# A routed MLP after sliding attention: the fourth unit's token rows gathered in quarters and turned by VectorE

## The chip, the cores and the metric

The kernel runs on one core of one Trainium2 chip. The metric is the device time of one execution in microseconds (us). The core has TensorE (matmuls), VectorE, ScalarE, GpSimd and SyncE, which run side by side and meet at semaphores, and sixteen DMA engines that move data between the chip's large memory (DRAM) and the on-chip memory.

## What is computed

Attention with two masks (a window of 32 keys, or every fourth key of the last 128), then a mixture of 8 experts of which each token uses one. A token whose local gate is 0.5 or more takes the expert of the token before it. Batch 8, 8 heads of 64, 576 tokens, so 4608 token rows of D = 512; an expert is 512 to 1024 to 512.

```python
scores = np.where(masks[None], scale * np.matmul(q, k.transpose(0, 1, 3, 2)), -1e9)
attn = softmax(scores)
x = (attn @ v) as (B, S, H * D)
logits, local_gate = x @ w_gate, sigmoid(x @ w_local)
for b in range(B):
    prev_e = -1
    for s in range(S):
        fresh_e = argmax(logits[b, s])
        e = fresh_e if s == 0 or local_gate[b, s] < 0.5 else prev_e
        prev_e = e
        out[b, s] = softmax(logits[b, s])[e] * (relu(x[b, s] @ w1[e]) @ w2[e])
```

## The kernel before

**Stages.** For the first 150 us or so the kernel computes attention for 64 (batch, head) pairs and stores the rows x into a DRAM buffer `xd`. Routing (logits, the running expert, counts) is mixed in. Then come 24 *units* of the expert MLP, numbered from 0. Units 0 and 1 are formed early, from the first half of the tokens; all others are late, from all tokens. A *pair* unit holds two tiles of 128 tokens of one expert, a *full* unit one tile, a *half* unit 64 tokens. Units 0 to 4 and 6 are pairs, unit 5 is full. Weights sit in three slots; units 0, 2, 4 use slot 0, units 1, 3, 6 slot 1, unit 5 slot 2. The loop at L1333 runs, for each unit u: the first layer of u (`run_hidden`, L1268), the rows of u + 1 (`features`, L951), the gathers of u + 5, and the second layer of u - 1 (`run_output`, L1283).

**One layer of a pair** is seven products instead of eight (`chain`, L955): sums of weight blocks and of row blocks are made by VectorE (L869 to L878), TensorE makes the products in three banks x, y, z, and each bank is read out by `keep` (ScalarE) or `finish` (VectorE at L1037 for the first layer and L1118 for the second). Bank x collects several products; the last of them may only be added to it when VectorE's `finish` of the one before has read it.

**The rows of a unit** are gathered from `xd` by GpSimd's indirect DMAs (L910), a list of closures (`fetches`) that is worked off as the program is written out: each gap between products adds credit, and a gather costs 2 or 3 of it (`fetch_some`, L913). Whatever is missing is issued when the rows are needed (`fetch_all`, L921). Each gather is preceded by a one-element memset on VectorE (L909), for which GpSimd waits, so the place of that memset in VectorE's queue sets the earliest time of the gather.

**Two ways to turn rows.** A matmul needs rows with the features on the partitions. For units below `TURNED`, two gathers per tile of 128 tokens fetch half rows of 1 KB (256 features), by the indices `row0` and `row1`. TensorE turns them with four 128 by 128 transposes a tile (L942), and ScalarE copies the result (L943). For the other units, four gathers per tile fetch quarter rows of 512 bytes, by the indices `at`, each group of 32 partitions another quarter, so that VectorE's transpose of 32 by 32 squares (L936) puts everything in place by itself. The features then lie in another order, so these units use a second copy of the first weights, with its rows in that order (`w1[u >= TURNED]`, L821). A weight load is skipped when the slot already holds the expert (L826), except where the copy changes between a slot's two users (L822).

**When gathers are queued.** `late_tokens` (L1184) queues units FIRST to TURNED - 1 and `places` (L730), which computes `at`, queues units TURNED to 5. The rows of unit 3 are turned within the first layer of unit 2, after the fifth product (L1275).

VectorE's and TensorE's queues run in the order in which the program is written; nothing moves an instruction ahead later.

Of the kernel before, what the change touches and what calls it, by code (L numbers as in the profile page):

```python
# [73 lines left out]
EARLY, FIRST = 2, 2  # L74
# [7 lines left out]
KEPT = EARLY * GB * 2  # L82


TURNED = FIRST + 2

AHEAD = 4

# [117 lines left out]
def whole(ctx, tc, exact, bad, qk, v, wgl, w1, w2, con, msk, qmk, out, cst, wg, ones):  # L206
# [523 lines left out]
    def places():  # L730
# [13 lines left out]
        nc.vector.scalar_tensor_tensor(at, codes, a_code, high, Alu.mult, Alu.add)  # L744
        for u in range(TURNED, FIRST + AHEAD):
            gather(u)
# [54 lines left out]
    def of_unit(u, what, j=0, rows=P):  # L801
        return tiles[what, units[u]["late"]][:rows, units[u]["col"] + j:units[u]["col"] + j + 1]
# [8 lines left out]
    def weights(u, second):  # L811
# [8 lines left out]
        e, held = units[u]["expert"], units[u]["held"]  # L820
        w, s, pattern = (w2, raw2, "p m f -> p (m f)") if second else (w1[u >= TURNED], raw1, "p m k f -> p (m k f)")  # L821
        if not second and u >= TURNED and units[u]["before"] < TURNED:  # L822
            held = None
# [68 lines left out]
    def gather(u):  # L892


        for j, n in enumerate({"pair": (NQS, NQS), "full": (NQS,), "half": (ROW // SQ,)}[units[u]["kind"]]):
            for q in range(2 if u < TURNED else n):
                fetches.append((u, lambda u=u, j=j, q=q: fetch(u, j, q)))

    def fetch(u, j, q):
        late, col = units[u]["late"], units[u]["col"] + j  # L900
        if q == 0:
            shape = [P, 2, D // 2]
            xg[u, j] = (stage.tile(shape, F32, name="xg", bufs=8) if late else mw.tile(shape, F32, name="xg"))
        x = xg[u, j]
        if u < TURNED:
            to, of, place = x[:, q], xh if late else xh[:EARLY * GS * 2], of_unit(u, f"row{q}", j)
        else:
            to, of, place = x.rearrange("p g (q f) -> p (g q) f", f=P)[:, q], xq, tiles["at"][:, q, col:col + 1]
        nc.vector.memset(to[0:1, 0:1], 0.0)  # L909
        nc.gpsimd.indirect_dma_start(out=to, out_offset=None, in_=of,  # L910
                                     in_offset=bass.IndirectOffsetOnAxis(ap=place, axis=0))

    def fetch_some(time):  # L913

        since[0] = min(since[0] + time, 5)
        cost = 2 if fetches and FIRST <= fetches[0][0] <= TURNED else 3
        if fetches and since[0] >= cost:
# [502 lines left out]
```

## Time and profile before

| what | value |
|---|---|
| median of 3 runs | 655.15 us (655.09 to 656.98) |
| the profiled execution | 657.47 us |
| its span, first to last instruction | 655.7 us |
| mean granted TensorE clock | 0.995 |
| gathers of `xg` by GpSimd (L910) | 16 by `row`, 120 by `at` |
| weight loads (L827) | 48 issued, 2048 KB each |
| software DMA queue (gathers and stores) | 19.41 MB |

How to read the views: the chain of waits goes back from the last instruction to whatever released it, step by step. In the timeline each row is a start in us from the span's beginning, a length, an engine, a line of the program and what it writes and reads; in square brackets stand the idle time of that engine before it and what ended it. "PE" is TensorE, "DVE" VectorE, "ACT" ScalarE, "POOL" GpSimd, "SP" SyncE.

### The profile page before, as it was taken

To read this page: it belongs to the slowest core of one execution; us is meant where nothing else is said; L and a number is where in the kernel's file an instruction comes from. 1 tells how busy PE (TensorE), PEld (TensorE's weight loads), DVE (VectorE), ACT (ScalarE), POOL (GpSimd) and SP (SyncE) were. 2 spreads that over 40 slices of the span, in tenths; PEclk is the share of its full clock that TensorE was granted. 3 is DMA by queue.
4 is the path that set the end of the run, shared out by engine and by line. 5 is a ranking of instruction groups with operands and counts; after the bars stand their busy time and mean duration, and the time that the engine had idled before them with its cause. 6 is when DMAs were issued, how large, how long until landed. Compare 5 with 4: busy or idle time off the path is not lost.

```text
span 655.7 us, 14698 instructions
## 1 busy us (share of the span) xinstructions
PE 635.9 (97%) x5980; PEld 558.3 (85%) x5980; DVE 415.8 (63%) x963; ACT 177.9 (27%) x318; POOL 253.3 (39%) x242
## 2 busy tenths in 40 slices
PE   8999999998998999999999999999999999999995
PEld 7978898878887999999699998699997799997974
DVE  4758888888686486754819744639724749717451
ACT  3545444353111332212122112132112123112310
POOL 4332243124004646554755554427553443110011
PEclk9999999999998999999999999999999999999999
DMA  9999989497004698575624425544114555531201
GB/s 340 411 414 339 351 303 296 161 379 282 8 25 177 208 409 310 178 293 185 267 81 156 168 64 227 228 174 158 41 60 153 194 220 216 173 146 26 117 33 44
DMA packets 29020, 131.40 MB, mean 200 GB/s; under 512 B 4909, under 2 KB 15277, under 8 KB 23184
## 3 DMA queue, kind: packets, MB, share of 16 engines
q1 hardware_dynamic: 21200, 110.96, 45.4%
q0 software_dynamic: 7744, 19.41, 8.8%
q8 instruction: 49, 0.80, 0.5%
q14 instruction: 27, 0.22, 0.1%
HBM read 145.03 MB, written 19.40 MB: 251 GB/s over the span
## 4 chain that ended last, share of the span: by engine, by line
PE 84%; DVE 8%; DMA 4%; issue 2%; POOL 1%; ACT 0%; POOLq 0%; DVEq 0%
PE yp L1103 28%; PE hp L1027 26%; PE sc L325 6%; PE hp L1001 4%; PE pv L379 4%; PE yp L1091 4%; PE yp L1074 2%; PE hp L989 2%; PE tp L398 2%; DMA xg<-xd,row 2%; DMA kq<-in_qk_dram 1%; DMA vt<-in_v_dram 1%; PE ap L614 1%; DVE pr L331 1%; PE lp L428 1%
## 5 line engine op out<-in xcount | busy, mean ns | idle before, releaser
L910 POOL DMA_INDIRECT xg<-xd,at x120 | 136.4, 1137 | 140.5 <-DVE xg L909 114.3
L1062 POOL DMA_INDIRECT out_dram<-y,tok x36 | 48.6, 1351 | 122.2 <-DVE y L1118 65.0
L1037 DVE TENSOR_TENSOR h<-hp,h 128x512 f32<-128x512 f32 x45 | 31.0, 690 | 93.5 <-PE hp L1027 93.3
L1103 PE MATMUL yp<-sum,hc 128*128 128x256 f32 x384 | 88.5, 380 | 0.0
L1027 PE MATMUL hp<-xc,sum 128*128 128x128 f32 x720 | 85.6, 275 | 0.0
L1027 PEld LDWEIGHTS hp<-xc,sum 128*128 128x128 f32 x720 | 82.9, 192 | 0.1
L1103 PEld LDWEIGHTS yp<-sum,hc 128*128 128x128 f32 x384 | 72.8, 190 | 9.9
L1118 DVE SCALAR_TENSOR_TENSOR y<-yp,gate,y 128x256 f32<-128x256 f32 x48 | 23.2, 483 | 76.3 <-issue 46.1
L331 DVE SCALAR_TENSOR_TENSOR pr<-sc,mk 96x512 f32<-96x512 f32 x64 | 47.0, 748 | 23.0 <-PE sc L325 22.4
L1103 PE MATMUL yp<-raw,h 128*128 128x256 f32 x256 | 61.0, 381 | 0.0
L334 ACT ACTIVATE pr<-pr 96x512 f32<-96x512 f32 x64 | 43.8, 684 | 58.6 <-DVE pr L331 57.0
L325 PE MATMUL sc<-kq 64*96 64x64 f32 x1152 | 56.7, 248 | 2.4 <-issue 1.4
L1027 PE MATMUL hp<-xe,raw 128*128 128x128 f32 x480 | 58.8, 276 | 0.0
L1027 PEld LDWEIGHTS hp<-xe,raw 128*128 128x128 f32 x480 | 56.5, 192 | 1.9 <-issue 1.6
L325 PEld LDWEIGHTS sc<-kq 64*96 64x96 f32 x1152 | 52.1, 161 | 6.9 <-issue 3.0
L274 POOL COPY vt<-vt 32x585 f32<-32x585 f32 x48 | 33.5, 699 | 62.2 <-DMA vt<-in_v_dram 43.2
L1103 PEld LDWEIGHTS yp<-raw,h 128*128 128x128 f32 x256 | 47.4, 190 | 9.1 <-issue 3.2
L1031 ACT COPY h<-hp 128x512 f32<-128x512 f32 x45 | 26.3, 585 | 73.4 <-PE hp L1027 73.4
L1038 ACT ACTIVATE h<-h 128x512 f32<-128x512 f32 x45 | 28.4, 630 | 63.4 <-DVE h L1037 48.5
L379 PE MATMUL pv<-vt,pr 128*64 128x65 f32 x1152 | 41.9, 225 | 2.0 <-issue 1.6
L379 PEld LDWEIGHTS pv<-vt,pr 128*64 128x64 f32 x1152 | 37.0, 137 | 4.5 <-issue 1.9
L1111 ACT ACTIVATE y<-yp,gate 128x256 f32<-128x256 f32 x48 | 22.7, 473 | 59.9 <-PE yp L1103 59.9
(224 smaller groups left out, 955.6 us busy)
## 6 DMA issues: line engine op xcount, KB each, us to landing
raw<-in_w_dram SPq DMA_DIRECT2D x48, 2048.0 KB
kq<-in_qk_dram SPq DMA_DIRECT2D x13, 1184.0 KB
vt<-in_v_dram SPq DMA_DIRECT2D x15, 880.0 KB
xd<-x SPq DMA_DIRECT2D x16, 512.0 KB
kq<-in_qk_dram SPq DMA_DIRECT2D x6, 592.0 KB
xg<-xd,at POOLq DMA_INDIRECT x120
xd<-x SPq DMA_DIRECT2D x32, 32.0 KB
vt<-in_v_dram SPq DMA_DIRECT2D x1, 585.0 KB
```

Source lines behind the costliest of these rows:

```text
L274: nc.gpsimd.tensor_copy(t[k * WIN:(k + 1) * WIN, VQ:], t[KW:, k * NB * VW:(k + 1) * NB * VW])
L325: nc.tensor.matmul(sc[:KW, u, (i - a) * QB:(i - a + 1) * QB], lhsT=kt[h, i * QB:i * QB + KW], rhs=qt[h, i * QB:(i + 1) * QB], start=True, ...
L331: nc.vector.scalar_tensor_tensor(to, sc[:KW, :, :w], -CEIL, mk[:, at:at + w].unsqueeze(1).to_broadcast([KW, 2, w]), Alu.max, Alu.min)
L334: nc.scalar.activation(to, to, Act.Exp, scale=SCALE)
L379: nc.tensor.matmul(pv[half * QB:(half + 1) * QB, k - a], lhsT=pr[:, u, (i - a) * QB:(i - a + 1) * QB], rhs=vt[:, u, i], start=True, stop=T ...
L910: nc.gpsimd.indirect_dma_start(out=to, out_offset=None, in_=of, in_offset=bass.IndirectOffsetOnAxis(ap=place, axis=0))
L1027: nc.tensor.matmul(to[:, m], lhsT=a[:, m, kk], rhs=b[:, kk], start=first and m == 0 and kk == 0, stop=(kk == DK // 2 - 1), skip_group_chec ...
L1031: nc.scalar.copy(at((0, 1, 3)[k]), of)
L1037: nc.vector.tensor_tensor(at(k), of, at(k), op=Alu.add)
L1038: nc.scalar.activation(at(k), at(k), Act.Relu)
L1062: nc.gpsimd.indirect_dma_start(out=rows_of_out(), out_offset=bass.IndirectOffsetOnAxis(ap=of_unit(u, "tok", j), axis=0), in_=y, in_offset= ...
L1103: nc.tensor.matmul(to, lhsT=a[:, m], rhs=b[:, m], start=first and m == 0, stop=(m == FK // 2 - 1), skip_group_check=True)
```

## The change

One constant moves. `TURNED` is the number of the first unit whose rows come in quarters; it goes from 4 to 3, so that unit 3, the fourth, changes sides.

```diff
-TURNED = FIRST + 2
+TURNED = FIRST + 1
```

It acts in six places. `gather` queues eight quarter gathers for unit 3 instead of four half gathers (the bytes are the same, 256 KB). `fetch` takes its indices from `at`, so its gathers are queued in `places` and no longer in `late_tokens`. `turn_rows` turns unit 3 with two VectorE transposes instead of eight TensorE transposes and two ScalarE copies. `weights` loads unit 3's first weights from the second copy, without the condition on the expert, and unit 6's with it. `fetch_some` charges unit 4's gathers 3 instead of 2.

On VectorE, within the first layer of unit 2. `h` is that layer's result, read out of the banks `hp`; `xc` and `xe` belong to unit 3's rows. Before, `xg_3060` and `xg_3109` are the two tiles of unit 4:

```order
L1037 TENSOR_TENSOR h_3047<-hp_3050,h_3047 128x4x128
L876 TENSOR_TENSOR sum_1_2509<-raw2_0_78,sum_1_2509 128x1024
L909 MEMSET xg_3060 1x1
L1037 TENSOR_TENSOR h_3047<-hp_3048,h_3047 128x4x128
L909 MEMSET xg_3109 1x1
L1037 TENSOR_TENSOR h_3047<-hp_3049,h_3047 128x4x128
L909 MEMSET xg_3109 1x1 x2
L875 TENSOR_TENSOR xc_3152<-xe_3112 128x256
```

After the change, where `xg_2996` and `xg_3059` are the tiles of unit 3 and `xg_3108` is the first of unit 4:

```order
L1037 TENSOR_TENSOR h_3046<-hp_3049,h_3046 128x4x128
L876 TENSOR_TENSOR sum_1_2509<-raw2_0_78,sum_1_2509 128x1024
L909 MEMSET xg_3059 1x1
L1037 TENSOR_TENSOR h_3046<-hp_3047,h_3046 128x4x128
L909 MEMSET xg_3108 1x1
L936 STREAM_TRANSPOSE xe_3111<-xg_2996 128x4x128
L936 STREAM_TRANSPOSE xe_3111<-xg_3059 128x4x128
L1037 TENSOR_TENSOR h_3046<-hp_3048,h_3046 128x4x128
L909 MEMSET xg_3108 1x1 x2
L875 TENSOR_TENSOR xc_3141<-xe_3111 128x256
```

The two transposes stand between the second and the third addition, and the memsets there belong to tiles of one place earlier.

On VectorE, within the first layer of unit 3, up to the transposes of unit 4's rows. Before, with `xg_3193` the tile of unit 5 and `xg_3253` the first of unit 6:

```order
L877 TENSOR_TENSOR sum_1_2509<-raw2_0_78 128x1024
L909 MEMSET xg_3193 1x1
L871 TENSOR_TENSOR hc_2511<-h_3047 128x512
L909 MEMSET xg_3193 1x1
L1037 TENSOR_TENSOR h_3166<-hp_3169,h_3166 128x4x128
L872 TENSOR_TENSOR hc_2511<-h_3047,hc_2511 128x512
L909 MEMSET xg_3193 1x1
...
L878 TENSOR_TENSOR sum_1_2509<-raw2_0_78,sum_1_2509 128x1024
L909 MEMSET xg_3253 1x1
L936 STREAM_TRANSPOSE xe_3260<-xg_3060 128x4x128
L936 STREAM_TRANSPOSE xe_3260<-xg_3109 128x4x128
```

After, with `xg_3108` and `xg_3192` the tiles of unit 4:

```order
L877 TENSOR_TENSOR sum_1_2509<-raw2_0_78 128x1024
L909 MEMSET xg_3108 1x1
L871 TENSOR_TENSOR hc_2511<-h_3046 128x512
L909 MEMSET xg_3192 1x1
L1037 TENSOR_TENSOR h_3155<-hp_3158,h_3155 128x4x128
L872 TENSOR_TENSOR hc_2511<-h_3046,hc_2511 128x512
...
L878 TENSOR_TENSOR sum_1_2509<-raw2_0_78,sum_1_2509 128x1024
L909 MEMSET xg_3192 1x1
L936 STREAM_TRANSPOSE xe_3246<-xg_3108 128x4x128
L936 STREAM_TRANSPOSE xe_3246<-xg_3192 128x4x128
```

At this place the memsets that were those of units 5 and 6 are those of unit 4, up to the last, which stands directly ahead of the transposes that read its tile.

On GpSimd, the gathers and stores in the order in which they are issued, from the first gather of unit 3 on (`y` is the result of unit 1 that is stored). Before:

```order
L910 DMA xg_2996<-xd_67,row01_2883 128x256
L910 DMA xg_2996<-xd_67,row11_2884 128x256
L1062 DMA out_dram<-y_2923,tok0_2126 4608x512
L910 DMA xg_3032<-xd_67,row01_2883 128x256
L910 DMA xg_3032<-xd_67,row11_2884 128x256
L1062 DMA out_dram<-y_2924,tok0_2126 4608x512
L910 DMA xg_3060<-xd_67,at_2965 128x128 x4
L910 DMA xg_3109<-xd_67,at_2965 128x128 x4
```

After:

```order
L910 DMA xg_2996<-xd_67,at_2965 128x128 x2
L1062 DMA out_dram<-y_2923,tok0_2126 4608x512
L910 DMA xg_2996<-xd_67,at_2965 128x128 x2
L1062 DMA out_dram<-y_2924,tok0_2126 4608x512
L910 DMA xg_3059<-xd_67,at_2965 128x128 x4
L910 DMA xg_3108<-xd_67,at_2965 128x128 x4
L910 DMA xg_3192<-xd_67,at_2965 128x128 x4
```

Unit 3 takes the four places that unit 4's first tile had, and unit 4's two tiles follow four places later.

## The prediction

> **What bounds the kernel now.** First the shares of the page, then the chain of waits that ended last.
>
> ```profile
> span 655.7 us, 14698 instructions
> PE 635.9 (97%) x5980; PEld 558.3 (85%) x5980; DVE 415.8 (63%) x963; ACT 177.9 (27%) x318; POOL 253.3 (39%) x242
> PE 84%; DVE 8%; DMA 4%; issue 2%; POOL 1%; ACT 0%; POOLq 0%; DVEq 0%
> ```
>
> TensorE is busy 97% of the span and carries 84% of the chain. So TensorE time that goes is worth its length only where TensorE itself is what comes last, and a wait that reaches TensorE costs its full length. The chain in order of time (start, length, what) around units 2 and 3:
>
> ```profile
> 142.24 6.76 DMA xg<-xd,row
> ...
> 205.52 3.33 DMA xg<-xd,row
> ...
> 223.47 0.87 PE tp L942 x8
> 224.34 3.59 PE hp L1027 x32
> ...
> 238.32 0.62 DVE h L1037
> 238.98 2.05 PE hp L1027 x16
> 241.03 12.09 PE yp L1103 x56
> 253.12 12.50 PE hp L1027 x112
> ```
>
> The eight transposes of unit 3 (L942) are on the chain, 0.87 us. Between 228 and 239 the chain runs over VectorE, and from 238.98 on it stays on TensorE with units back to back: output of unit 2 at 241.03, hidden of unit 4 at 253.12. What is lost there is not won back.
>
> **The change, part by part.** *TensorE* loses the eight transposes, 0.87 us, and ScalarE their two copies, which nobody waits for after 228. *VectorE* gets two square transposes for unit 3, in its queue behind the second of unit 2's three additions at L1037 and ahead of the third. *GpSimd* issues eight gathers for unit 3 where it issued four, so every later gather moves four places back. The rows of VectorE (start, length, idle time before it and what ended it):
>
> ```profile
> 223.58 0.69 DVE L1037 TENSOR_TENSOR h<-hp,h 128x512 f32<-128x512 f32 x1
> 226.17 0.69 DVE L1037 TENSOR_TENSOR h<-hp,h 128x512 f32<-128x512 f32 x1 [1.90 <-PE hp L1027]
> 228.03 0.43 DVE L875 TENSOR_TENSOR xc<-xe 128x256 f32<-128x256 f32 x1 [1.16 <-PE hp L1027]
> 235.25 1.22 DVE L877 TENSOR_TENSOR sum<-raw 128x1024 f32<-128x1024 f32 x1
> 240.64 0.71 DVE L936 STREAM_TRANSPOSE xe<-xg 128x512 f32<-128x512 f32 x1
> 242.92 0.71 DVE L936 STREAM_TRANSPOSE xe<-xg 128x512 f32<-128x512 f32 x1 [1.58 <-DMA xg<-xd,at]
> 250.29 0.48 DVE L1118 SCALAR_TENSOR_TENSOR y<-yp,gate,y 128x256 f32<-128x256 f32 x1
> ```
>
> and of GpSimd's gathers:
>
> ```profile
> 223.89 0.94 POOL L910 DMA_INDIRECT xg<-xd,at  x1 [0.90 <-DVE xg L909]
> 235.94 1.35 POOL L910 DMA_INDIRECT xg<-xd,at  x1 [5.53 <-DVE xg L909]
> 241.83 0.94 POOL L910 DMA_INDIRECT xg<-xd,at  x1 [0.30 <-issue]
> ```
>
> *Unit 3.* Its two transposes cost 2 x 0.71 = 1.4 us, and the idle 1.90 + 1.16 us before 226.17 and 228.03 covers that, if the data is there. Counting GpSimd's queue, unit 3's eighth gather takes the place that starts at 223.89. Under light traffic a gather took 3.33 us from its start until TensorE had it (205.52). Its issue had taken 1.61 us of that and this one takes 0.94, so I take 2.66, and the second transpose starts at 226.55. The third addition then runs 227.25 to 227.9, and xc (L875) starts at 227.95 instead of 228.03. TensorE comes 0.87 us earlier and then waits for VectorE's sums, which come 0.1 us earlier: of the 0.87 us about 0.1 is left. The bounds: all of the 0.87 gained if the data is early, or a gather of the loaded kind (142.24: 6.76 us; and 235.94 to 242.92, 6.98 us), landing at 230.87 and making VectorE 4.2 us late. I stay with the light case, for the load between 225 and 230 is light (busy time of each engine in a stretch; the last three columns are TensorE's granted clock, the busy share of the DMA engines and GB/s):
>
> ```profile
> 200.00:205.00 5.00, 5.00 (x25) 4.41 (x24) 4.57 (x13) 0.95 (x2) 2.55 (x2) 1.00 0.83 350
> 225.00:230.00 5.00, 5.00 (x46) 4.87 (x45) 2.67 (x7) 1.97 (x5) 3.48 (x3) 1.00 0.39 85
> 235.00:240.00 5.00, 4.85 (x44) 4.66 (x43) 5.00 (x13) 1.66 (x3) 3.24 (x3) 1.00 0.98 416
> 240.00:245.00 5.00, 5.00 (x30) 4.51 (x29) 3.28 (x8) 1.77 (x4) 3.33 (x3) 1.00 1.00 411
> 245.00:250.00 5.00, 5.00 (x25) 4.41 (x24) 4.97 (x8) 0.48 (x2) 1.72 (x2) 1.00 1.02 415
> ```
>
> *Unit 4* is where I expect the price. Now only one of its eight gathers is late: it starts at 235.94, and VectorE waits 1.58 us for it, until 242.92. After the change five are left at that point. The first of them has its memset behind L877 (235.25 + 1.22), so it starts at about 236.5, and the last has its memset right ahead of the transposes. GpSimd's five starts from 235.94 to 241.83 lie (241.83 - 235.94) / 4 = 1.47 us apart, so the last of unit 4's starts at 236.5 + 5.9 = 242.4. From 235 to 250 the DMA engines are full with weights (0.98 to 1.02), so I take 6.5 us for the landing, just under the 6.76 and 6.98 measured under load, since the load ends near 250. The bounds are 3.33 and 6.98. It lands at 248.9, and VectorE's second transpose starts 6.0 us late (248.9 against 242.92).
>
> Who waits: behind it stand unit 4's xc and weight sums and then the additions of unit 2's output at L1118. The one at 250.29 ends at 250.77, and TensorE's last product of that output writes on in the bank that it reads:
>
> ```profile
> 249.51 1.89 PE L1103 MATMUL yp<-raw,hc 128*128 128x256 f32 x8
> 251.23 1.89 PE L1103 MATMUL yp<-sum,h 128*128 128x256 f32 x8
> ```
>
> The slack is 251.23 - 250.77 = 0.46 us. Six us later the addition ends at 256.75, and TensorE stands **256.75 - 251.23 = 5.5 us** behind, with nothing else in its queue. The 0.87 us that it saved lies ahead of that stall and is swallowed by it.
>
> *Clock.* After an idle stretch the granted clock can halve:
>
> ```profile
> 148.00:149.00 1.00, 0.00 (x0) 0.00 (x0) 1.00 (x2) 0.00 (x0) 0.00 (x0) 1.00 1.16 457
> 210.00:211.00 1.00, 1.00 (x4) 0.73 (x4) 0.85 (x3) 0.09 (x1) 0.00 (x0) 0.50 0.45 131
> ```
>
> and on TensorE just ahead of the second of them:
>
> ```profile
> 208.99 0.47 PE L942 MATMUL tp<-cst,xg 128*128 128x128 f32 x2 [1.43 <-DMA xg<-xd,row]
> 209.26 3.55 PE L1103 MATMUL yp<-raw,hc 128*128 128x256 f32 x8
> ```
>
> After 1.43 us idle eight matmuls took 3.55 us instead of 1.89, at a clock of 0.50; a similar pause around 148.5 left it at 1.00. A pause of 5.5 us is far longer than either, so I add 3.55 - 1.89 = **1.7 us**. The Trainium skill (TensorE: Matmul & The Clock Gate, Part 1) has the clock halve after an idle window of about 3.4 us that runs freely. By that rule a pause of 5.5 us would be hit in most phases but not in all, 1.7 us with or without; the trace shows a drop after less idle time than it asks for.
>
> *Priced at nothing:* unit 3's first weights come from the other half of the weight table, 2 MB either way; that this load runs now is seen in the 350 GB/s at 200 to 205. Its condition on the expert held goes, and unit 6's load gets one; by the reference's inputs the slot's experts are 1, 4 and 5, so both load in both kernels. If unit 6's were skipped, the load from 241 on would thin, which is the light rival below.
>
> **Sum.** 5.5 + 1.7 = 7.2 us, on the profiled execution's span of 655.7 (its time 657.47). The median of the runs, 655.15, lies 2.3 us under that execution's time, with nothing that the change touches in between, so I add to the median: **662.3 us**.
>
> **Rivals.**
>
> 1. *The clock holds.* Only the stall: 655.15 + 5.5 = 660.7. For it speaks the row at 148.
> 2. *The late gather lands as under light load.* 242.4 + 3.33 = 245.7, 2.8 us late, so the addition ends at 253.6 and TensorE loses 2.4 us, a pause too short to be sure of a slow clock: 657.5. Against it stand the three windows at 0.98 to 1.02. The Trainium skill (DMA: Bandwidth & Descriptors, Anatomy of one DMA) gives 2.0 us and the bytes over 436 GB/s, by its figure an estimate of 2.15 us for 64 KB, so this rival is its rule. The 6.98 us here speaks against it.
> 3. *VectorE is never late* (not slower). If unit 4's last gather had landed by 242.92 + 0.46 = 243.4, no wait would reach TensorE, and at most the 0.87 us would remain: 654.3. It decides at a landing 1.0 us after the start at 242.4. No gather quoted was that quick.
> 4. *Unit 3's own last gather comes late as well* (weights for unit 4 start early and load the queue). VectorE is 4.2 us late at xc, TensorE waits there with a slow clock (1.7), and unit 4's gathers move by the same 4.2: together some 4.2 + 7.2 = 11.4 us, 666.5. Against it speaks 0.39 at 225 to 230.
>
> **How the numbers follow.** The forecast 0.62, rival 1 0.13, rival 2 0.11, rival 3 0.05, rival 4 0.09. The range 657.0 to 664.5 takes in landings from 3.3 to about 8 us with and without the clock, and leaves out rival 3, the lower part of rival 2 and rival 4, together about 0.18. A measurement of this kernel tells some 0.3% (2 us) from no change, 653.2 to 657.1: within it lie most of rival 3 and a third of rival 2, 0.08; faster 0.02; slower 0.90.
>
> **What would show it.** Right: no L942 near 223; the second unit-3 transpose on VectorE ending near 227; a wait of several us at unit 4's L936 for DMA xg, ending near 249; TensorE's last product of unit 2's output (L1103, now at 251.23) waiting for VectorE's L1118 until near 257, then some 3 us at half clock, and from there on every unit at its old length. Wrong: L936 of unit 4 released before 244; TensorE idle at 228 to 231, which would be rival 4; or a new wait at units 5 or 6, whose gathers also shift but whose last memsets stand 18 and more rows of VectorE's queue ahead of their transposes.

## The result, and the profile after

| | kernel before | changed kernel |
|---|---|---|
| median, 4 runs each on one chip | 655.88 us (655.09 to 656.98) | 665.47 us (662.10 to 666.52) |
| profiled execution, its span | 657.47, 655.7 us | 665.62, 663.8 us |
| mean granted clock | 0.995 | 0.993 |

The ratio is 1.0137, with a 95% interval of 1.0113 to 1.0160. On the 655.15 us from which the forecast was made this is 664.1 us (662.6 to 665.6), a loss of 9.0 us where 7.2 was forecast. The changed kernel's own median, 665.47, lies 1.0 us over the upper end of the range. One execution of `eager` below, 929 us at a granted clock of 0.654, is left out of its times.

The shares of the page, after:

```profile
span 663.8 us, 14702 instructions
PE 640.4 (96%) x5972; PEld 562.4 (85%) x5972; DVE 417.7 (63%) x969; ACT 176.8 (27%) x316; POOL 255.0 (38%) x246
PE 81%; DVE 9%; issue 4%; DMA 3%; POOL 2%; ACT 0%; POOLq 0%; DVEq 0%
```

TensorE has fewer instructions and yet is busy 4.5 us longer. That is not the price of the change: 3.0 us of it lie in the attention scores (L325, 59.7 us against 56.7), which the change doesn't touch, and the changed kernel's second trace, `after_2`, has 56.7 there again. What counts is that its share of the chain falls from 84% to 81%: elsewhere it waits.

The chain of waits in order of time (start, length, what):

```profile
242.63 6.94 DMA xg<-xd,at
249.75 0.72 DVE xe L936
...
256.06 1.13 DVE sum L872
257.65 3.78 PE yp L1103 x8
261.43 13.04 PE hp L1027 x112
274.48 12.09 PE yp L1103 x56
...
625.24 12.09 PE yp L1103 x56
```

A gather (xg) has taken TensorE's place on the chain. The output of unit 4 starts at 274.48, and that of the last units at 625.24. In the chain of the kernel before:

```profile
265.63 12.09 PE yp L1103 x56
...
616.39 12.09 PE yp L1103 x56
```

Both are 8.85 us earlier there. So nothing is lost or won in the 350 us behind the first of them; all of it happens ahead of 274. (The spans differ by 8.1 us only, because from the issue of the last store to the end it takes 4.8 us here and 5.5 before.) TensorE, from the timeline (idle time and what ended it in brackets):

```profile
230.31 3.81 PE L1027 MATMUL hp<-xc,sum 128*128 128x128 f32 x32 [0.73 <-DVE sum L869]
...
250.05 1.89 PE L1103 MATMUL yp<-raw,hc 128*128 128x256 f32 x8
257.65 3.78 PE L1103 MATMUL yp<-sum,h 128*128 128x256 f32 x8 [5.71 <-DVE xg L909]
```

The last but one product of unit 2's output starts at 250.05, against 249.51 before. Up to there the two executions differ by 0.54 us only. That is a balance: the first product of any unit's output (L1103) starts 2.36 us later than before (168.27 against 165.91), before loses 1.66 us to its half clock near 209, and of the 0.87 us saved some 0.2 are left. The last product starts at 257.65; with before's distance of 1.72 us it would be 251.77, so **5.88 us** are lost at the stop. That product then takes 3.78 us instead of 1.89, and the first layer of unit 4 takes 13.04 instead of 12.50: **2.43 us** more. 0.54 + 5.88 + 2.43 = 8.85, of which 5.88 + 2.43 = 8.31 belong to the change.

The name in the bracket, the memset L909, is a neighbour in VectorE's queue; what TensorE waits for is seen in VectorE's own rows:

```profile
224.96 0.70 DVE L936 STREAM_TRANSPOSE xe<-xg 128x512 f32<-128x512 f32 x1
227.33 0.71 DVE L936 STREAM_TRANSPOSE xe<-xg 128x512 f32<-128x512 f32 x1 [1.67 <-issue]
228.56 0.42 DVE L875 TENSOR_TENSOR xc<-xe 128x256 f32<-128x256 f32 x1
...
244.51 0.71 DVE L936 STREAM_TRANSPOSE xe<-xg 128x512 f32<-128x512 f32 x1 [3.12 <-DMA xg<-xd,at]
249.75 0.71 DVE L936 STREAM_TRANSPOSE xe<-xg 128x512 f32<-128x512 f32 x1 [4.53 <-DMA xg<-xd,at]
...
255.58 0.48 DVE L1118 SCALAR_TENSOR_TENSOR y<-yp,gate,y 128x256 f32<-128x256 f32 x1
257.11 0.48 DVE L1118 SCALAR_TENSOR_TENSOR y<-yp,gate,y 128x256 f32<-128x256 f32 x1
```

VectorE waits 3.12 and 4.53 us for unit 4's two tiles, and the additions at L1118 that release TensorE's bank run at 255.58 and 257.11 instead of about 250. The clock around that (busy times of the engines; the last three columns are granted clock, busy share of the DMA engines and GB/s):

```profile
245.00:250.00 5.00, 5.00 (x25) 4.41 (x24) 0.47 (x2) 0.95 (x2) 0.00 (x0) 1.00 1.01 413
...
256.00:257.00 1.00, 0.00 (x0) 0.00 (x0) 1.00 (x2) 0.00 (x0) 0.58 (x1) 0.50 1.11 475
...
261.00:262.00 1.00, 1.00 (x6) 0.91 (x5) 1.00 (x2) 0.47 (x1) 1.00 (x1) 0.50 0.27 66
```

The gather lands while the DMA engines are full (1.01), and the clock goes to half during the stop and stays there past the last product, in this execution.

### The profile page after: what moved, and what is told of

It reads as the page before. It is cut to its first block, busy times and chain, and to the rows that moved or that the text cites. A ratio compares the mean times of both kernels' runs of the same rounds, so it can differ in the third digit from the quotient of the medians.

```text
span 663.8 us, 14702 instructions
## 1 busy us (share of the span) xinstructions
PE 640.4 (96%) x5972; PEld 562.4 (85%) x5972; DVE 417.7 (63%) x969; ACT 176.8 (27%) x316; POOL 255.0 (38%) x246
## 4 chain that ended last, share of the span: by engine, by line
PE 81%; DVE 9%; issue 4%; DMA 3%; POOL 2%; ACT 0%; POOLq 0%; DVEq 0%
PE yp L1103 26%; PE hp L1027 25%; PE sc L325 7%; PE pv L379 5%; PE hp L1001 4%; PE yp L1091 4%; PE yp L1074 2%; PE hp L989 2%; PE tp L398 2%; DMA kq<-in_qk_dram 2%; POOL xg L910 1%; DMA xg<-xd,at 1%; PE ap L614 1%; DVE pr L331 1%; PE lp L435 1%
## 5 line engine op out<-in xcount | busy, mean ns | idle before, releaser
L910 POOL DMA_INDIRECT xg<-xd,at x128 | 140.4, 1097 | 147.0 <-DVE xg L909 121.0
L1062 POOL DMA_INDIRECT out_dram<-y,tok x36 | 50.1, 1392 | 121.4 <-DVE y L1118 63.9
L1103 PE MATMUL yp<-sum,hc 128*128 128x256 f32 x384 | 88.5, 380 | 0.0
L1027 PE MATMUL hp<-xc,sum 128*128 128x128 f32 x720 | 85.6, 275 | 0.7 <-DVE sum L869 0.7
L1027 PEld LDWEIGHTS hp<-xc,sum 128*128 128x128 f32 x720 | 82.9, 192 | 0.9 <-PE hp L1027 0.9
L1103 PEld LDWEIGHTS yp<-sum,hc 128*128 128x128 f32 x384 | 72.9, 190 | 9.8
L1118 DVE SCALAR_TENSOR_TENSOR y<-yp,gate,y 128x256 f32<-128x256 f32 x48 | 23.1, 483 | 74.2 <-issue 47.7
L325 PE MATMUL sc<-kq 64*96 64x64 f32 x1152 | 59.7, 258 | 1.4 <-DVE pr L331 0.6
L1103 PE MATMUL yp<-raw,h 128*128 128x256 f32 x256 | 61.0, 381 | 0.0
L325 PEld LDWEIGHTS sc<-kq 64*96 64x96 f32 x1152 | 55.4, 171 | 5.7 <-issue 1.4
L1027 PE MATMUL hp<-xe,raw 128*128 128x128 f32 x480 | 59.4, 278 | 0.0
L1027 PEld LDWEIGHTS hp<-xe,raw 128*128 128x128 f32 x480 | 57.3, 194 | 2.1 <-issue 1.2
L1103 PEld LDWEIGHTS yp<-raw,h 128*128 128x128 f32 x256 | 47.4, 190 | 9.0 <-issue 3.2
L1031 ACT COPY h<-hp 128x512 f32<-128x512 f32 x45 | 26.3, 586 | 73.8 <-PE hp L1027 73.8
```

The costliest lines, as they stand in the source:

```text
L325: nc.tensor.matmul(sc[:KW, u, (i - a) * QB:(i - a + 1) * QB], lhsT=kt[h, i * QB:i * QB + KW], rhs=qt[h, i * QB:(i + 1) * QB], start=True, ...
L1027: nc.tensor.matmul(to[:, m], lhsT=a[:, m, kk], rhs=b[:, kk], start=first and m == 0 and kk == 0, stop=(kk == DK // 2 - 1), skip_group_chec ...
L1062: nc.gpsimd.indirect_dma_start(out=rows_of_out(), out_offset=bass.IndirectOffsetOnAxis(ap=of_unit(u, "tok", j), axis=0), in_=y, in_offset= ...
L1103: nc.tensor.matmul(to, lhsT=a[:, m], rhs=b[:, m], start=first and m == 0, stop=(m == FK // 2 - 1), skip_group_check=True)
```

## The experiments

The kernels ran on several chips, each time beside the kernel before on the same chip, and the chips fall into two kinds. On chip 5 the kernel before takes 654.57 us; on chips 0, 2, 6 and 12 it takes 665.17, 666.01, 664.68 and 665.25. The change costs 1.4% on the first kind and 2.5% on the second (chip 0). So each result is read against its own chip. **Theory A**: the loss comes from the places of unit 4's gathers, and from the half clock after the stop. **Rival B**: it comes from turning on VectorE, or from the work that TensorE lacks.

**The two kernels again.** `before_again` and `after_again` on chip 0, `after_2` on chip 5.

> The kernel before, once more, to see how much its executions differ where the change does nothing. In the first two profiles the last memset ahead of unit 2's second gather stood at 196.73 us before and 199.08 us after the change, 2.35 us apart, although no instruction up to there differs; and the clock fell to 0.50 at 210 only before. Theory A (both are differences between executions): this profile has another start of that place than 196.73, or another clock at 210, and its times spread over 655 to 657. Theory B (the change slows the early stages too): that place stays at 196.5 to 197.0 in every execution of before, and the 2.35 us belong to the change.

> The changed kernel, once more, for its interval and a second trace. Theory A: the wait of TensorE before the last product of unit 2's output (5.71 us idle in the first profile) and the half clock behind it (to 262.5 us) come back within 0.5 us, and what else differs between executions differs without them: time 662 to 666.5, 7.5 to 9.5 us over before. Theory B: the early stages are 2 us late again, at 199 us for unit 2's first memsets.

> The changed kernel once more, as the measure for the three others. In the last job before was some 10 us slower than in the first and the changed kernel lost 16 us on it, with further stops of TensorE of 1 to 3.5 us (at 313, 349, 416 and 451 us) that no semaphore of the profile ends and that fall some 10 us behind a packet of the instruction queue q8. Theory A alone (the late gather of unit 4, with the slow clock): 7.5 to 9.5 us over before where those stops are missing. Theory C (beside A, code that reaches TensorE late, at other places in the changed kernel than before, since 8 transposes less shift the 16 KB blocks): wherever before shows such stops, the changed kernel shows others, and the difference to before is 8 us plus the difference of those stops.

> The kernel before, for a second trace on a chip where it takes about 655 us (the times of a job hang on its chip: 655 twice, 665 once). Theory A: no idle time of TensorE over 2 us behind 200 us; the drop of the clock near 208 (1.7 us) is there in some executions and not in others, so its times fall into two groups 1.5 to 2 us apart, 653.5 to 655 and 656 to 657.

`before_again` 663.63 us and, on chip 2, `before_3` 666.24, both within 0.3% of the kernel before beside them; `after_again` 681.75 (ratio 1.0247, 1.0229 to 1.0266); `after_2` 664.40 (1.0141, 1.0106 to 1.0175). So `after_2` repeats the first comparison. On chip 0 the stop ahead of the last product is 3.44 us long, shorter than expected, and something is added that the first trace doesn't have; it is taken up last. Theory B of these texts, that the change slows the early stages, falls: the first product at L1103 starts at 165.91 and 164.99 in two traces of the kernel before, at 168.27 in the changed kernel's first trace and at 164.04 in `after_2`. Executions differ there by 4 us with nothing changed.

**Only the places: `padded`.** The kernel before, with four gathers into a tile that nobody reads, ahead of unit 4's; unit 3 is still turned by TensorE.

```diff
...
+            fetches.extend((TURNED - 1, lambda q=q: spare_gather(q)) for q in range(NQS))
...
-        cost = 2 if fetches and FIRST <= fetches[0][0] <= TURNED else 3
+        cost = 2 if fetches and FIRST <= fetches[0][0] < TURNED else 3
```

> The kernel before (unit 3 in half rows, turned by TensorE) with four more quarter gathers behind unit 3's into a tile that nobody reads, and the changed kernel's credit for unit 4, so that unit 4's gathers stand where the change puts them. Theory A: the loss belongs to the places of unit 4's gathers: TensorE stands idle 4 to 7 us before the last product of unit 2's output, the clock halves, and the time is 7 to 10 us over before. Rival (the turning by VectorE or unit 3's own gathers): no such wait, within 2 us of before.

664.52 us on chip 5 (1.0137, 1.011 to 1.0165), the time of the changed kernel. Its timeline, VectorE's transpose of unit 4's second tile and TensorE's last product of unit 2's output (the added lines move L936 to L946 and L1103 to L1113):

```profile
248.93 0.71 DVE L946 STREAM_TRANSPOSE xe<-xg 128x512 f32<-128x512 f32 x1 [6.14 <-DMA xg<-xd,at]
```

```profile
256.82 3.78 PE L1113 MATMUL yp<-sum,h 128*128 128x256 f32 x8 [6.77 <-DVE xg L919]
```

Not one row more is turned on VectorE, TensorE has all its work, and wait, stop and half clock are all there. Rival B falls: the places are enough. (The four added gathers move 256 KB that the changed kernel doesn't. Unit 3 itself takes 256 KB for each of its two tiles, 512 KB in either form.)

**The 0.87 us given back: `idle_turns`.** The changed kernel, with eight transposes of a constant on TensorE where unit 3's stood.

```diff
+                if u == FIRST + 1:
+                    tp = bank([P, DK, P], "tp")
+                    for kk in range(DK):
+                        nc.tensor.transpose(tp[:, kk], ones, ident)
```

> The changed kernel with eight transposes of a constant on TensorE where unit 3's were, used by nobody, so that TensorE's program has the length of before from there on. Theory A: the wait at unit 4's transposes stays, and these cost nothing, for 0.87 us of work lies ahead of that wait: as the changed kernel within 0.5 us. Theory C: the stops behind 300 us return to the places and lengths of before, so that in a job like the last it is several us faster than the changed kernel (8 to 10 us over before instead of 16); in a job like the first no difference.

664.39 us on chip 5, against 664.40 for `after_2` beside it. Each median is of four runs that lie 3 to 5 us apart, so the trace has to say it. TensorE goes on without a wait where the changed kernel waits 0.73 us (230.31; the added lines move L1027 to L1031):

```profile
228.10 3.84 PE L1031 MATMUL hp<-xc,sum 128*128 128x128 f32 x32
```

The removed TensorE work is worth next to nothing there.

**The load: `light_2`.** The changed kernel, with both weight loads of unit 5 and the first of unit 6 issued later, so that the DMA engines are nearly idle when the late gather is under way. (`light`, the same kernel on chip 2: 679.98 us, 1.0212.)

```diff
-        if u == FIRST:
+        if u == FIRST + 1:
             weights(third, False)
...
-        elif after[u] is not None:
+        elif after[u] is not None and u != FIRST + 1:
             weights(after[u], False)
...
+            if u == FIRST:
+                weights(after[u + 1], False)
             weights(after[u], True)
```

> The changed kernel with three weight loads moved later on SP's queue: both of unit 5's and the first of unit 6's now stand behind unit 4's second load, which waits for the end of unit 2's output. The DMA engines are then nearly idle while unit 4's last gathers land. Theory A (the landing under load is what makes the last gather late): it lands about 3 us after its start instead of 7, the wait at unit 4's second transpose falls from 4.5 to 5.7 us to at most 2, TensorE stands 1 to 3 us instead of 5.7 to 6.7, and the time is 3 to 6 us under the changed kernel, if the moved loads come in time for units 5 and 6. Rival (the gather is late because of its place on GpSimd alone): the landing stays near 7 us, and so does the wait.

> The weights of the third stage are loaded one unit later, so unit 4's late gather lands under light DMA load. On a chip where before takes about 655 us: theory A gives a landing of 2.7 to 3.4 us, a stall of 0.6 to 2.4 us instead of 5.7 to 6.8, and 655.5 to 659 us. Rival B (the loss is in the turning on VectorE or the missing TensorE work) gives the time of the changed kernel, about 664. On a chip at 666: +12 to +15 us from the other stops, whichever holds at unit 4.

674.82 us on chip 6 (1.0135, 1.01 to 1.0171). The time is mixed with other stops of that chip; the place itself is clear. GpSimd's last gather of unit 4, VectorE's transpose of it, TensorE's last product of unit 2's output, and two windows:

```profile
242.53 0.94 POOL L910 DMA_INDIRECT xg<-xd,at  x1 [0.30 <-issue]
```

```profile
245.19 0.71 DVE L936 STREAM_TRANSPOSE xe<-xg 128x512 f32<-128x512 f32 x1 [3.27 <-issue]
```

```profile
253.10 1.99 PE L1103 MATMUL yp<-sum,h 128*128 128x256 f32 x8 [0.73 <-DVE xg L909]
```

```profile
240.00:245.00 5.00, 4.93 (x30) 4.17 (x28) 1.92 (x5) 1.60 (x4) 2.83 (x3) 1.00 0.18 52
245.00:250.00 5.00, 4.81 (x22) 4.27 (x23) 4.63 (x10) 0.98 (x3) 1.00 (x1) 1.00 0.01 3
```

The gather starts at 242.53, as in the changed kernel (242.63), but its data is used 2.66 us later instead of 7.12. The stop shrinks to 0.73 us, and the eight matmuls run at full clock. `idle_turns_2`, the changed kernel with idle transposes on the same chip, stops 6.84 us there and takes 684.45 us, 9.6 more. So the late gather costs what it does because it lands among weights. The Trainium skill (DMA: Bandwidth & Descriptors, Anatomy of one DMA) gives 2.0 us plus the bytes over 436 GB/s, by its figure an estimate of 2.15 us for 64 KB: near the 2.66 of the idle queue (0.94 of them the issue), far from the 7.12 of the full one.

**The clock: `filled27_2`.** The changed kernel with matmuls on a constant in the wait, so that TensorE never idles there.

```diff
+            if u == FIRST and k == 5:
+                to = bank([P, P], "fill")
+                for _ in range(27):
+                    nc.tensor.matmul(to, lhsT=ones, rhs=ones, start=True, stop=True)
```

> The changed kernel with 27 matmuls (54 passes, about 6 us) on constants in the wait ahead of the last product of unit 2's output. On a chip at 655: if the half clock costs what the profile shows (1.6 to 2.4 us), the time is 1.5 to 2.5 us under the changed kernel, about 662 to 663, with a granted clock of 1.00 from 250 to 265; rival: the clock would be halved at another place anyway, and the time stays at 664 to 665.5. On a chip at 666 the fill is longer than the wait, and the time says little.

678.59 us on chip 6 (1.0189, 1.016 to 1.0217). TensorE, and the window:

```profile
253.41 6.19 PE L1292 MATMUL fill<-ones 128*128 128x128 f32 x54
259.44 1.89 PE L1103 MATMUL yp<-sum,h 128*128 128x256 f32 x8
```

```profile
255.00:260.00 5.00, 5.00 (x45) 4.95 (x44) 5.00 (x12) 0.00 (x0) 3.37 (x3) 1.00 0.87 358
```

The clock stays at 1.00 and the product takes 1.89 us. (The fill outlasts by some 0.7 us the addition that TensorE waits for, and the other stops of this chip differ as well, so the trace is read here and not the time.) `idle_turns_2`, on the same chip, has the stop unfilled:

```profile
259.05 3.78 PE L1107 MATMUL yp<-sum,h 128*128 128x256 f32 x8 [6.84 <-DVE xg L909]
```

On the chains of waits the way from that product to the output of unit 4 is 14.64 us with the fill (259.44 to 274.08) and 16.96 without (259.05 to 276.01). In this pair the half clock costs **2.3 us**, where 1.7 was put down. It isn't so everywhere. In `after_2` the same way, from the product's start to the output of unit 4, takes 271.60 - 255.58 = 16.02 us:

```profile
247.46 1.89 PE L1103 MATMUL yp<-raw,hc 128*128 128x256 f32 x8
255.58 3.52 PE L1103 MATMUL yp<-sum,h 128*128 128x256 f32 x8 [6.23 <-DVE xg L909]
271.60 12.09 PE yp L1103 x56
```

Against the 14.40 us of the kernel before (251.23 to 265.63) that is 1.62 us for the clock, and 2.43 in the first trace. `padded` (2.54) and `idle_turns` (1.70) differ in the same way. The windows at the two ends of the half clock show why, first the changed kernel's first trace, then `after_2`:

```profile
255.00:256.00 1.00, 0.00 (x0) 0.00 (x0) 1.00 (x3) 0.00 (x0) 0.69 (x2) 0.80 0.88 377
262.00:263.00 1.00, 1.00 (x9) 1.00 (x8) 0.10 (x2) 0.00 (x0) 0.69 (x2) 0.78 0.07 29
```

```profile
251.00:252.00 1.00, 0.00 (x0) 0.00 (x0) 0.97 (x3) 0.00 (x0) 0.52 (x1) 0.93 0.58 197
258.00:259.00 1.00, 1.00 (x5) 0.81 (x4) 1.00 (x2) 0.00 (x0) 0.69 (x2) 0.65 0.00 0
```

A clock of 0.80 in one microsecond is half clock for 0.4 of it. So the half clock goes from 255.6 to 262.4 in the one and from 251.9 to 258.7 in the other: 6.8 us in both. What it costs is half of the part that falls on work: 4.8 us behind 257.65, but only 3.1 behind 255.58. Added up over windows of 0.25 us, it lasts 3.41 us after the short pause near 209 in the kernel before, 3.41 after 1.92 us in `filled15`, 6.83 after the stops of 5.71 to 6.84 us in five traces (the two above, `padded`, `idle_turns`, `idle_turns_2`), and 10.24 after the 8.32 us of `eager_4`: each a multiple of 3.41.

The pauses that set it off differ: 1.92 us were enough in `filled15`, 0.73 in `light_2` were not, and a pause of about 1.45 us near 209 halves it in some executions of either kernel (before's profiled one, `after_2`) and not in others (after's first, 1.48 us). The Trainium skill (TensorE: Matmul & The Clock Gate, Part 1) asks for an idle window of about 3.4 us that runs freely. That the same pause halves the clock in some executions only fits a window that runs freely; that 1.4 to 1.9 us were enough doesn't fit its length.

Two fills missed. `filled` (44 matmuls, chip 0) was longer than the wait: 685.16 us (1.0286), later than the changed kernel beside it. `filled27` on chip 2 overshot too, since the addition that TensorE waits for ended some 2 us ahead of the fill there: 685.54 (1.0285). `filled15` on chip 5 left 1.92 us idle, kept the half clock and came to 662.58 (1.013, 1.0083 to 1.0178), which can't be told from 664.40.

> The changed kernel with 44 matmuls of a constant (about 4.9 us at full clock) put into TensorE's queue ahead of the last product of unit 2's output, where it stands idle 5.71 us; their result is used by nobody. The late gather and the wait stay. Theory A: the clock stays at 1.00 there, so the 2.4 us that the half clock costs (the last product 3.78 instead of 1.89, the layer behind it 13.04 instead of 12.50) go and the 5.7 us stay: about 2.4 us under the changed kernel, some 6 us over before. Rival (the clock is no part of it, the loss is the wait alone): no difference from the changed kernel.

> The changed kernel with 15 matmuls of a constant (30 passes, about 3.35 us at full clock; the 44 of the first try were 88 passes and 9.8 us, longer than the wait) ahead of the last product of unit 2's output. Theory A: of the 5.7 us (3.4 in the last job) of idle time at most 2.4 us are left, the clock stays at 1.00 there, the last product takes 1.9 instead of 3.5 to 3.8 us and the layer behind it 12.5 instead of 12.7 to 13.0: 1.8 to 2.4 us under the changed kernel of this job. Rival (the clock costs nothing): no difference from the changed kernel.

> The changed kernel with 27 matmuls of a constant (54 passes, about 6.0 us) ahead of the last product of unit 2's output; with 15 of them TensorE still stood 1.9 us and the clock still halved. The expectation for that run was too high: what keeps the clock is that hardly any idle time is left. Theory A: idle time under 1 us there, granted clock 1.00 from 245 to 262, the last product 1.9 us and the layer behind it 12.5 us: 1.5 to 2.4 us under the changed kernel, 6.5 to 8 us over before. Rival (the clock falls for another reason, or costs nothing): the half clock stays, or the time does.

**The places given back: `eager`.** The changed kernel, with the gathers of units 3 and 4 charged 1 instead of 3, two to a gap, so that unit 4's last memset again stands well ahead of its transposes.

```diff
-        cost = 2 if fetches and FIRST <= fetches[0][0] <= TURNED else 3
-        if fetches and since[0] >= cost:
+        for _ in range(2):
+            at = fetches[0][0] if fetches else NU
+            cost = 1 if at in (FIRST + 1, FIRST + 2) else 2 if at == FIRST else 3
+            if not fetches or since[0] < cost:
+                break
             since[0] -= cost
             fetches.pop(0)[1]()
+            if cost > 1:
+                break
```

> The changed kernel with another credit in the list of gathers: units 3 and 4 cost 1 and up to two gathers go per gap, so the memsets of unit 4's last gather stand about 13 us of VectorE work ahead of its transposes instead of directly ahead. Theory A (the late gather of unit 4 is the whole loss): no wait at unit 4's transposes, TensorE has no idle 5.7 us at 252, no half clock there, and the time is that of before or up to 0.9 us less: 654 to 657, 8 to 9 us under the changed kernel. Rival (the two transposes on VectorE, or unit 3's doubled gathers, cost by themselves): 2 us or more over before stay. Theory B (2 us are lost early): 657 to 659.

> The changed kernel with gathers of units 3 and 4 issued early, again; in its first job, where before took 665 us, the wait at unit 4's transposes was gone and TensorE instead stood 5.5 us at 226 us and 3.5 us at 348 us, 10 us behind packets of the instruction queue. Theory A: on a chip where before takes 655 us these stops are small or missing, unit 4's transposes do not wait, and the time is 653.5 to 656, at most 1 us over and up to 1 us under before, 8 to 10 us under the changed kernel. Rival (the closer burst of gathers holds up TensorE's code on every chip): a stop of TensorE near 222 to 228 us again, 5 us or more over before.

> Unit 4's gathers are issued where they stood before, at most two to a gap, and unit 3 still turns on VectorE. On a chip where the kernel before takes about 655 us: theory A (the loss is the late last gather of unit 4, and the clock after it) gives 653.5 to 656.5 us, no wait over 1 us ahead of the last product of unit 2's output, and full clock there. Rival (GpSimd's gathers back to back cost a wait of their own, or a stop of TensorE) gives 3 to 9 us over before, with the wait at 224 to 235 us. On a chip where before takes about 666 us the rival's stop is expected again, +12 to +15 us.

> As eager_3. On a chip where before takes about 655 us: 653.5 to 656.5 by theory A, 3 to 9 us over before by its rival (a wait of GpSimd's at 224 to 235 us). On a chip at 665: a stop of 4 to 9 us at 226 to 231, none ahead of the last product of unit 2's output, and 10 to 15 us over before.

It met only chips of the second kind: 678.00 us (chip 0, ratio 1.0191), 680.52 (`eager_2`, chip 2, 1.0221), 676.62 (`eager_3`, chip 6, 1.0177), 674.62 (`eager_4`, chip 12, 1.0134, 1.0088 to 1.0179). In `eager_4` VectorE turns unit 4 without a wait, in one row:

```profile
250.78 1.30 DVE L941 STREAM_TRANSPOSE xe<-xg 128x512 f32<-128x512 f32 x2
```

and TensorE has no stop near 250 to 260. But it has another, earlier:

```profile
229.40 3.78 PE L1032 MATMUL hp<-xc,sum 128*128 128x128 f32 x16 [8.32 <-issue]
```

So the place of the gathers removes the wait, as theory A says, and the rival's stop is there too: about as much is lost again at another place.

**The other stops: `padded_2` and `idle_turns_2`.** On the second kind of chip TensorE stops for 0.6 to 9 us where no semaphore explains it ("issue", or a ScalarE step long done). The kernel before has such a stop, here on chip 2 (`before_3`):

```profile
341.68 3.32 PE L1027 MATMUL hp<-xc,sum 128*128 128x128 f32 x16 [4.22 <-ACT h L1031]
```

with 0.77 us more at 227 and 1.28 at 541; `after_again` has them at 313 (1.17 us), 349 (3.44), 416 (1.17), 451 (2.98) and 554 (0.66). One theory was that they stand at fixed lengths of TensorE's program, which the change shortens; the rival, that they follow the gathers.

> The changed kernel with eight transposes of a constant on TensorE where the change took them away. On a chip at 655: the time of the changed kernel, about 664.4 (as idle_turns). On a chip at 666: theory C (the stops that no semaphore ends stand at fixed lengths of TensorE's program) has the large stops back near 343 and 542 us (4 us and 1 us) as in the kernel before, and +8 to +10 us over before; the rival (they follow GpSimd's gathers in time, whatever TensorE's program) has them near 313, 349, 415 and 451 us as in the changed kernel, and +14 to +16 us.

> The kernel before, with four gathers into an unread tile that move unit 4's and all later gathers to the places they have after the change. On a chip where before takes about 655 us: 664 to 665, the wait of 6 to 7 us at the last product of unit 2's output (as padded). On a chip at 665: if the places of the gathers set the other stops, they stand near 313, 349, 416 and 451 us as in the changed kernel, and the time is 14 to 18 us over before; the rival (they follow something else that the change moves, the turning on VectorE or TensorE's shorter program) has them near 341 and 540 us as before, and 7 to 9 us over before.

`idle_turns_2` has TensorE's length of before and the gathers of after: 684.45 us (1.0283, 1.0245 to 1.0322), stops at 316, 353, 420, 455 and 558, as after the change. `padded_2` has all of TensorE's and VectorE's work of before; only four gathers with their memsets are added, which moves the gathers behind them: 680.80 us on chip 12 (1.0237, 1.0197 to 1.0277), the loss of the changed kernel on chip 0. Its stops:

```profile
311.10 2.05 PE L1037 MATMUL hp<-xc,sum 128*128 128x128 f32 x16 [1.19 <-ACT h L1041]
...
347.05 2.52 PE L1037 MATMUL hp<-xc,sum 128*128 128x128 f32 x16 [3.46 <-issue]
413.79 2.05 PE L1037 MATMUL hp<-xc,sum 128*128 128x128 f32 x16 [1.14 <-ACT h L1041]
449.15 2.05 PE L1037 MATMUL hp<-xc,sum 128*128 128x128 f32 x16 [2.98 <-issue]
```

The theory of the program's length falls. Where the stops stand is set by where the gathers stand.

## Why the prediction came out short

- **Where and why.** The place (last product of unit 2's output), the carrier (unit 4's second tile at L936, then L1118) and the swallowed 0.87 us came as written, and `padded`, `light_2` and `idle_turns` show each by itself. From there on the units keep their old length.
- **Unit 3.** The light landing was right: the second transpose starts 2.63 us after its gather (224.70 to 227.33; put at 2.66), and TensorE waits 0.73 us for VectorE's sums. Rival 4 didn't come.
- **The step that failed** is the size of the sum's two terms, 5.5 + 1.7 = 7.2 us. From the last but one product of unit 2's output to the output of unit 4 the kernel before takes 16.12 us (249.51 to 265.63), the changed kernel 24.43 and in `after_2` 24.14 (247.46 to 271.60). So the two terms together measured **8.31** and **8.02 us**.
- **"5.5 us" of the stop** measured 5.88 in the first trace and 6.40 in `after_2`. The landing was put too low: 6.5 us, where the chains of waits have 6.94 and 7.46. The value just under the loaded rows was a choice; the loaded rows themselves were nearer. That the gather started almost where it was put (242.09 with the executions' 0.54 us taken off, against 242.4) was partly luck: the run of five began 0.6 us later than put, and its starts lay 1.25 us apart instead of 1.47.
- **"1.7 us" of the clock** measured 2.43 in the first trace, 2.3 by `filled27_2` and 1.62 in `after_2`. It was read off a short pause, whose half clock lasted 3.41 us, all of it on work. After the long stop it lasts 6.83 us and begins within the stop, so the cost depends on where it falls. Where 1.7 fitted, it fitted by luck.
- **The rest.** The ratio gives 9.0, with an interval (7.4 to 10.5) that holds 8.0 and 8.3 and just misses 7.2. Against 655.88, the median beside it, the changed kernel's median is 9.6 us up. Of the 3.2 us between 662.3 and 665.47, so, 0.7 are a higher median of the kernel before in the comparison, 1.1 the two terms in the first trace, and 1.3 are not explained. They are less than what executions differ by: the four runs are 4.4 us apart, and the first product at L1103 starts up to 4.2 us apart in two traces of the changed kernel.
- **The range** took its upper end from a landing of about 8 us with the clock term unchanged, and left no room for a half clock that costs more or for the runs' own spread.
- **Not foreseen at all**: a second kind of chip, where the same change costs some 16 us. The trace of before shows no such stop, so nothing in it could have said so.

What stays open: whether `eager` returns the whole loss on a chip like the first, where it didn't run; and what TensorE waits for in the other stops. No version tried was faster than the kernel before.

## What to carry to other kernels

When a change puts entries into a queue that is worked off in order, price the last entry that is pushed right up to its consumer, not the one that was changed: here the fourth unit was altered and the fifth paid. Take a late transfer's landing from rows under the same load (7 us here against 2.7 with the DMA engines idle). And don't carry the price of the half clock over from a shorter pause: here it lasted 3.4 us after a short one and 6.8 us after the long stop, and it costs half of the part that falls on work.

## What the hardware showed that was not expected

The stops of the second kind of chip stand where GpSimd issues gathers and stores one after the other with 0.3 us between them. In `before_3`, from the first to the last row of such a run of ten:

```profile
326.73 0.97 POOL L910 DMA_INDIRECT xg<-xd,at  x1 [0.30 <-issue]
...
338.38 0.97 POOL L910 DMA_INDIRECT xg<-xd,at  x1 [0.30 <-issue]
```

One packet of 16 KB on the queue for instructions goes at 331, and TensorE stands until 341.68, 2.3 us after the run of gathers ends. In `padded_2` such a run ends at 346.18 and TensorE resumes at 347.05; in `eager_4` one ends at 227.97 and TensorE resumes at 229.40. On chip 5 `after_2` issues such a run from 331.54 to 344.88, with its packet at 336, and has no stop there. That TensorE's instructions come late while GpSimd issues gathers fits these rows, but it was only argued: no run took the packet away, and in `eager_3` TensorE resumes at 226.09, before the run of gathers ends.
